# A list-scheduled attention and MLP kernel: the planner's lengths, its ranks, the order of transfers and the gates of the weights are replaced

## The chip, the core and the metric

The kernel runs on one core of a Trainium2 chip. A core has five engines that each run their own instruction queue strictly in order: TensorE (PE in the profile, with PEld for its weight loads), VectorE (DVE), ScalarE (ACT), GpSimd (POOL) and SyncE (SP), which here only issues DMAs. The engines meet through semaphores. DMA transfers run on 16 DMA engines beside them; SP's and ACT's go through one kind of queue (hardware_dynamic, q1 and q10 in the profile), POOL's through another (software_dynamic, q0). The metric is the device time of one execution in microseconds; the median of three runs is the kernel's time.

## What is computed

Four batches of eight heads, 768 positions, head size 64. Keys are cut into 24 chunks of 32. For each query an upper bound of its score with each chunk is worked out, the six best chunks that are not in the future are kept, and attention runs over those alone. The result, seen as 3072 tokens of 512 numbers, goes through an MLP with a hard-swish.

```python
ub = sum(max(q * k_min[chunk], q * k_max[chunk]))          # per query and chunk
ub = where(causal, ub, -1e9); top = argsort(ub)[..., -6:]
scores = where(sel & (pos_q >= pos_k), q @ k.T / 8, -1e9)
attn = softmax(scores) @ v                                  # -> x: 3072 x 512
h = x @ w_in                                                # 512 -> 2048
out = (h * clip(h + 3, 0, 6) / 6) @ w_out                   # 2048 -> 512
```

## The kernel before

**Tiling.** The 32 heads make 16 pairs, p0 to p15; a batch b has four pairs, and two pairs make a quad that is loaded together. The 768 positions are handled in two halves of 384. A unit is two pairs and one half: unit 0 is p0, p1 in half 0; unit 1 is p2, p3 in half 0; units 2 and 3 are their half 1; units 4 and 5 are p4, p5 and p6, p7 in half 0, and so on to unit 15.

**Attention of a pair and half.** K and Q are loaded by SP. In batch 0 the load is `load_quad` (L237, rows of 768 bytes) and TensorE turns the tile (`turn`, L377); in the other batches it is `load` (L246): four transfers, each into 32 of the 128 partitions in rows of 128 bytes, and VectorE turns the tile by a transpose over all 128 partitions (`turn_out`, L389), so that this transpose needs all four transfers. Then come the chunk limits (`limits`, L402 and L403 on VectorE, L405), GpSimd's copies of keys and queries (L340, `keys` and `queries`), the bounds (L442), the selection on VectorE (L447 to L472, `largest`, `select`, `select_out`), the scores (L495 for batch 0, L498 for the others), the exponentials (L508 on ScalarE), the causal triangle (L513 on GpSimd), the product with V (`values`, L529) and its division (`values_out`, L535 and L541 on VectorE). V is loaded at L252 (batch 0, three transfers) or L257 and cast by `cast_values`.

**MLP of a group.** A group g is a batch and a half, 384 tokens; g00 is batch 0, half 0. Its tokens are turned by TensorE (`turn_tokens`, L550, copied out at L554) for g00, g01 and g10, and by VectorE and a round trip through DRAM for the other five (`turn_words` L560, `keep_words` L565, `fetch_words` L571, `part_words` L579 on GpSimd). Then come 16 `hidden` blocks (L586, each followed by L591 on ScalarE and L594 on VectorE) and three `result` tiles of four parts (L601; the last tile of all at L609). Each `hidden`, `values`, `turn`, `turn_tokens` or `result` tile takes one of four PSUM banks ("m"), and gives it back when the engine that reads it is done.

**Weights.** `load_weights` issues four transfers of 1 MB on GpSimd's queue: I0 and I1, the halves of w_in (needed by `hidden` blocks 0 to 7 and 8 to 15), and O0 and O1, the halves of w_out. Ahead of each stands a copy of one element of an earlier transfer's tile (`seen`, L322): the gate. GpSimd stands still at it until that transfer has landed. I0 to O1 are issued in this order.

**What sets the order.** Nothing above is written in its final order. The function body only registers steps with `plan.add`: an engine or several to choose from, a length in microseconds, a rank, the steps it follows, and the buffers it takes and gives back. `Plan.order` then plays a list schedule: at each moment a free engine takes the ready step of lowest rank. The instructions are emitted in that order, engine by engine, so that the plan decides every queue, but at run time only the semaphores hold anything back. `SHIFT` adds a number to the ranks of about 200 steps. A transfer is given a length too, and is stretched by a share while weights are under way:

```python
weights = max(free["WT"] - now, 0.0) + sum(x["lengths"]["WT"] for x in ready["WT"])
length = min(length / st["share"], weights + max(length - st["share"] * weights, 0.0))
```

Of the kernel before, what the change touches and what calls it, by code (L numbers as in the profile page):

```python
# [46 lines left out]
class Plan:  # L47
# [8 lines left out]
    FETCH = 15.3, 1.35  # L56
# [36 lines left out]
    def order(self, **busy):  # L93
# [20 lines left out]
        while events:  # L114
            now, _, done, own = heapq.heappop(events)
            if done:
                behind(done, own)
                if not own:
                    for held in done["give"]:
                        held[1] -= 1  # L120
                        if not held[1]:
                            self.room[held[0]].append(held[2])
                            opened[held[0], held[2]] = now
            for e, steps in ready.items():
                if free[e] > now + 1e-9:
                    continue
                for st in sorted(steps, key=lambda x: x["rank"][:1] if e == "DMA" else x["rank"]):
                    if "engine" in st:
                        steps.remove(st)
                    elif self.sooner(st, e, free, now):  # L130
                        continue
                    elif self.room_for(st):
                        steps.remove(st)
                        for held in st["take"]:
                            held[2] = self.take(held[0])
                        st["idle"] = now - max([free[e], *(opened.get((held[0], held[2]), 0.0) for held in st["take"])])
                        out.append(st)
                        begin = now
                        if e == "POOL" or e == "DVE" and st["port"]:
                            begin = max(now, port["DVE" if e == "POOL" else "POOL"])  # L140
                            port[e] = begin + st["lengths"][e]
                        begin = max(begin, locks.get(st["lock"], 0.0))
                        if e == "PE":
                            begin += 0.1 * (st["tiles"] != tiles)
                            tiles = st["tiles"]
                        length = st["lengths"][e]
                        if e == "PE" and begin < self.COLD:
                            length *= 1.9
                        if e == "DMA":
                            weights = max(free["WT"] - now, 0.0) + sum(x["lengths"]["WT"] for x in ready["WT"])  # L150
                            length = min(length / st["share"], weights + max(length - st["share"] * weights, 0.0))
                            if now <= self.FETCH[0] < now + length:
                                length += self.FETCH[1]
                        st["at"], st["engine"], st["length"] = begin, e, length
                        free[e] = begin + st["length"]
                        if st["lock"]:
                            locks[st["lock"]] = free[e] + 0.12
                        n += 2
                        heapq.heappush(events, (free[e], n, st, True))
                        heapq.heappush(events, (free[e] + self.BEHIND[e], n + 1, st, False))  # L160
                        break
# [10 lines left out]
def kernel(  # L172
# [465 lines left out]
    GATE = dict(I0="V3", I1="I0", O0="K4", O1="I1")  # L638
# [34 lines left out]
    def load_input(n, name, after=()):  # L673
# [17 lines left out]
        elif half == 0:  # L691
            got = arrive("SP", 0.6, 1.35, (load, two, name, x), after=after, take=take, parts=4)
            for st in two:
                there[name, st["pair"], 0] = there[name, st["pair"], 1] = got
# [42 lines left out]
    def prepare(n):  # L737
# [11 lines left out]
        for st in two:  # L749
# [3 lines left out]
            for name, f in (("KS", "kf"), ("QS", "qf")):  # L753
# [3 lines left out]
                if first:  # L757
                    m = bank_of[name] = hold("m", 2 if name == "KS" else 1)
                    here = direct[name] = [add("PE", 0.4, r + lead, later(turn, st, name, half), after=here, take=[m], give=used)]
# [9 lines left out]
            else:  # L769
                masks_beside(p, r)  # L770
                made["K", p, half] = [add(dict(POOL=0.54), None, r + lead + 1, later(keys, st, half, j), port=True,
                                          after=[a] + free.get(("KL", p - 6), []), give=[held["kf"]]) for j in range(2)]
            b1 = add("DVE", 0.95 if first else 0.93, r + lead, later(limits, st, half, 0), after=(direct["KS"] if first else [a]) + free.get(("KM", p - 6), []),
# [11 lines left out]
            chain += [c, add(dict(ACT=0.45, DVE=0.33, POOL=0.6) if first else dict(ACT=0.42), None, r + lead, later(queries, st, half, "relu"), after=[c], port=True,  # L785
# [4 lines left out]
            made["Q", p, half] = [add(dict(POOL=0.54), None, r + lead + 1, later(queries, st, half, j), port=True,  # L790
# [17 lines left out]
    def attend(u):  # L808
# [8 lines left out]
        a = add("DVE", 0.36 if half == 0 else 0.53, r + RANK["sel"], later(select, u), after=[a] + selected.get(half, []), give=[ub], port=True)  # L817
# [3 lines left out]
        for j in range(2 if n >= 4 else 0):  # L821
            mask.append(add(dict(DVE=0.46, ACT=0.83, POOL=0.9), None, r + RANK["sel"] + j, later(masks_out, u, j), port=True,
# [3 lines left out]
        for i, st in enumerate(two):  # L826
# [6 lines left out]
            for t in range(tiles):  # L833
# [12 lines left out]
                for jb, q0, w, c0 in PLAN[half][t]:  # L846
                    if q0 == jb * P:
                        parts.append(add("POOL", 0.37, r + RANK["tri"], later(triangle, st, half, t, c0), after=[e]))
# [43 lines left out]
    for what in ("I0", "I1", "O0", "O1"):  # L892
        name, n = dict(I="WIN", O="WOUT")[what[0]], int(what[1])
        got, seen = landing[GATE[what]]
        there[name, n] = arrive("POOL", 0.95, 6.3 if name == "WIN" else 7.3, (load_weights, name, n, seen), after=got[-1:])
# [3 lines left out]
    for n_group, ((b, half), xs) in enumerate(finished.items()):  # L899
# [3 lines left out]
        if (b, half) in WORDS:  # L903
# [12 lines left out]
            for kt in range(KT_HID):  # L916
                xt.append(add("POOL", 0.55, r + RANK["rw"], later(part_words, g, kt), after=landed + xt[:1], take=[held_xt] if kt == 0 else [], give=[held_bf]))
# [6 lines left out]
        for f in range(FT):  # L924
# [3 lines left out]
            a = add("ACT", 0.48, r + RANK["fs"] * f + RANK["rt"], later(hidden_relu, g, f), after=before, take=[u])  # L928
            gts.append(add("DVE", 0.475, r + RANK["fs"] * f + RANK["rt"], later(hidden_out, g, f), after=[a], give=[m, u]))
# [59 lines left out]
```

## Time and profile before

| | us |
|---|---|
| median of 3 runs (range) | 271.57 (270.55 to 271.87) |
| profiled execution, its own time | 270.71 |
| its span | 269.0 |
| PE busy | 258.5 (96%) |
| DVE busy | 205.2 (76%) |
| ACT busy | 190.0 (71%) |
| POOL busy | 125.6 (47%) |

The page gives shares for the whole span, and the timeline, the waits and the DMA view can be asked for a stretch of it. A line of a timeline is start, duration, engine, source line, operation, output and inputs, and the number of instructions merged into it; in brackets stands the idle time before it and what ended that. A line of the DMA view is the queue, its packets, megabytes and the time of its packets as a share of the 16 DMA engines in the stretch; under "issues" the last number is the microseconds from issue to landing. The granted TensorE clock was 0.998.

### The profile page before, as it was taken

The numbers are of one execution on the slowest core, as the hardware profiler recorded it, in microseconds if no ns is written. First come the engines' busy times: TensorE is split into PE (matmuls) and PEld (weight loads), VectorE is DVE, ScalarE is ACT, GpSimd is POOL, SyncE is SP. The second block draws the span as 40 slices with busy tenths as digits, with TensorE's granted clock in tenths as the row PEclk, the third lists the DMA queues.
The fourth block names the chain that finished last, engine by engine and source line by source line (L and its number), as shares of the span: only waits on it lengthen the run. The fifth ranks groups of instructions, "written<-read, shape, count | busy, mean of one in ns | idle before, by whom it ended". The sixth has DMA issues, their size and how long they took to land.

```text
span 269.0 us, 6720 instructions
## 1 busy us (share of the span) xinstructions
PE 258.5 (96%) x2466; PEld 155.2 (58%) x2484; DVE 205.2 (76%) x582; ACT 190.0 (71%) x305; POOL 125.6 (47%) x284
## 2 busy tenths in 40 slices
PE   7998999999999999899999999999999999999994
PEld 5855666665445666554664566644666556645553
DVE  5789889889988698799889999979997126804800
ACT  3777899686457788764994499944997679716810
POOL 2547577005958559648845584772372221111000
PEclk9999999999999999999999999999999999999999
DMA  7999999999982999994999799223100420042012
GB/s 222 286 208 177 176 180 193 200 131 146 221 208 84 145 177 168 132 175 138 140 143 167 178 130 174 54 80 117 40 0 4 156 80 1 2 157 80 0 39 78
DMA packets 115329, 34.91 MB, mean 130 GB/s; under 512 B 100960, under 2 KB 110688, under 8 KB 115296
## 3 DMA queue, kind: packets, MB, share of 16 engines
q1 hardware_dynamic: 111616, 29.89, 60.3%
q0 software_dynamic: 3136, 4.19, 9.5%
q8 instruction: 19, 0.31, 0.5%
q10 hardware_dynamic: 544, 0.39, 0.5%
q14 instruction: 14, 0.11, 0.1%
HBM read 29.23 MB, written 8.26 MB: 139 GB/s over the span
## 4 chain that ended last, share of the span: by engine, by line
PE 73%; DVE 8%; DMA 7%; ACT 4%; SPq 3%; issue 1%; POOL 1%; ACTq 0%; DVEq 0%; POOLq 0%
PE OP L601 24%; PE HP L586 23%; PE SPS L498 6%; DMA KS<-in_k_dram 5%; PE PVP L529 5%; PE UBT L442 5%; PE SPS L495 3%; DVE GT L594 3%; ACT PT L508 3%; PE QT L377 2%; PE KT L377 2%; SPq L246 2%; PE OP L609 1%; DVE KF L389 1%; DMA BD<-BT 1%
## 5 line engine op out<-in xcount | busy, mean ns | idle before, releaser
L508 ACT ACTIVATE PT<-SPS 128x1024 bf16<-128x1024 f32 (+2 forms) x96 | 84.5, 927 | 11.6 <-PE SPS L498 7.9
L586 PE MATMUL HP<-XT,WIN 128*128 128x384 bf16 x512 | 90.1, 326 | 1.3 <-DVE Xb L541 0.8
L594 DVE SCALAR_TENSOR_TENSOR GT<-U,HP 128x384 bf16<-128x384 bf16 x128 | 67.2, 549 | 29.9 <-ACT U L591 25.6
L601 PE MATMUL OP<-WOUT,GT 128*128 128x512 bf16 x350 | 83.4, 379 | 1.2 <-issue 0.3
L591 ACT ACTIVATE U<-HP,THREE 128x384 bf16<-128x384 f32 x128 | 71.6, 594 | 8.1 <-PE HP L586 4.2
L586 PEld LDWEIGHTS <-WIN 128*128 128x128 bf16 x512 | 48.8, 98 | 32.6 <-issue 1.3
L513 POOL TENSOR_SCALAR_AFFINE_SELECT PT<-PT 128x256 bf16<-128x256 bf16 x96 | 39.6, 423 | 51.5 <-ACT PT L508 50.7
L601 PEld LDWEIGHTS <-GT 128*128 128x128 bf16 x368 | 34.7, 98 | 40.4 <-issue 3.7
L340 POOL TENSOR_SCALAR_AFFINE_SELECT QLA<-QF 64x384 bf16<-64x384 f32 x48 | 24.2, 506 | 24.6 <-DVE QF L389 18.9
L498 PE MATMUL SPS<-QLA,KL 128*128 128x384 bf16 (+2 forms) x240 | 35.5, 278 | 0.1
L627 ACT ACTIVATE OT<-OP 128x512 f32<-128x512 f32 x22 | 13.1, 594 | 30.0 <-PE OP L601 26.7
L498 PEld LDWEIGHTS <-KL 128*128 128x128 bf16 x240 | 21.4, 98 | 12.1 <-issue 0.3
L340 POOL TENSOR_SCALAR_AFFINE_SELECT KL<-KF 64x384 bf16<-64x384 f32 x48 | 24.1, 504 | 8.3 <-DVE KF L389 6.7
L529 PEld LDWEIGHTS <-PT 128*128 128x128 bf16 x672 | 24.3, 97 | 6.0 <-POOL PT L513 2.4
L529 PE MATMUL PVP<-VB,PT 128*128 128x65 bf16 x672 | 26.3, 193 | 1.2 <-POOL PT L513 1.1
L413 ACT ACTIVATE QR<-QF 128x384 f32<-128x384 f32 x29 | 14.5, 525 | 10.4 <-DVE QF L389 8.5
L541 DVE TENSOR_TENSOR Xb<-PVP,RINV 128x384 bf16<-128x384 f32 x32 | 18.5, 579 | 1.1
L579 POOL COPY XT<-BF 128x384 bf16<-128x384 bf16 x20 | 9.7, 523 | 14.9 <-DMA BF<-BD 14.8
L389 DVE STREAM_TRANSPOSE KF<-KS 128x384 f32<-128x384 f32 x24 | 13.2, 560 | 3.3 <-DMA KS<-in_k_dram 3.3
L266 POOL TENSOR_SCALAR_AFFINE_SELECT VB<-VT 128x768 bf16<-128x768 f32 x12 | 10.8, 908 | 6.4 <-DMA VT<-in_v_dram 4.3
L389 DVE STREAM_TRANSPOSE QF<-QS 128x384 f32<-128x384 f32 x24 | 12.3, 550 | 1.7 <-PE UBT L442 1.7
L402 DVE TENSOR_REDUCE KMA<-KF 128x12 f32<-128x384 f32 x24 | 13.1, 547 | 0.5
(75 smaller groups left out, 223.6 us busy)
## 6 DMA issues: line engine op xcount, KB each, us to landing
KS<-in_k_dram SPq DMA_DIRECT2D x31, 192.0 KB, 5.2
QS<-in_q_dram SPq DMA_DIRECT2D x31, 192.0 KB, 5.5
out_dram<-OT SPq DMA_DIRECT2D x23, 256.0 KB, 2.2
VT<-in_v_dram SPq DMA_DIRECT2D x24, 192.0 KB, 4.6
WIN<-in_moe_w_in_dram POOLq DMA_DIRECT2D x2, 1024.0 KB, 9.3
WOUT<-in_moe_w_out_dram POOLq DMA_DIRECT2D x2, 1024.0 KB, 13.0
BD<-BT SPq DMA_DIRECT2D x5, 384.0 KB, 2.3
BF<-BD SPq DMA_DIRECT2D x20, 96.0 KB, 2.3
```

The costliest lines, as they stand in the source:

```text
L340: nc.gpsimd.affine_select(out=to, in_=x, pattern=[[0, n]], compare_op=A.is_ge, fill=0.0, base=0, channel_multiplier=0)
L389: nc.vector.transpose(T[:], st[name][:, st["i"], half * HC:(half + 1) * HC, :].rearrange("p c e -> p (c e)"))
L413: nc.scalar.activation(QR[:], QF[:], ACT.Relu)
L498: nc.tensor.matmul(SP[:, j, c0:c0 + n], lhsT=KLS[st["pair"] % 6][:, j, jb * P:(jb + 1) * P], rhs=st["QL", half][:, j, at:at + n], start=Tr ...
L508: nc.scalar.activation(PT[:, :, 0:cols], SP[:, :, 0:cols], ACT.Exp, scale=scale)
L513: nc.gpsimd.affine_select(out=PT[:, :, c0:c0 + P], in_=PT[:, :, c0:c0 + P], pattern=[[0, 2], [1, P]], compare_op=A.is_ge, fill=0.0, base=0 ...
L529: nc.tensor.matmul(PVP[:, j, n, :], lhsT=PT[:, j, c0:c0 + P], rhs=st["VB"][:, jb, j, :], start=(jb == 0), stop=(jb == qb))
L541: nc.vector.tensor_tensor(out=to, in0=PVP[:, :, :, 0:D], in1=RINV[:].to_broadcast([P, 2, HB, D]), op=A.mult)
L586: nc.tensor.matmul(HP[:], lhsT=WIN[:, kt, f * P:(f + 1) * P], rhs=g["XT"][:, kt, :, :], start=(kt == 0), stop=(kt == KT_HID - 1))
L591: nc.scalar.activation(U[:], g["HP", f][:], ACT.Relu, bias=THREE[:], scale=1.0)
L594: nc.vector.scalar_tensor_tensor(out=g["GT"][:, f, :], in0=g["U", f][:], scalar=6.0, in1=g["HP", f][:], op0=A.min, op1=A.mult)
L601: nc.tensor.matmul(g["OP", t][:], lhsT=g["GT"][:, f, t * P:(t + 1) * P], rhs=WOUT[:, f, :], start=(f == 0), stop=(f == FT - 1))
```

## The change

No instruction's work changes, and there are as many DMAs. What changes is the numbers from which the order is made:

- lengths of steps: the turns of batch 0 (0.4 to 0.65), several of GpSimd's (`keys` and `queries` 0.54 to 0.5, `part_words` 0.55 to 0.47, the triangle 0.37 to 0.39), `select`, `masks_out`, `hidden_relu`, the issue of weights (0.95 to 1.05), the four-part load (1.35 to 1.4);
- the instruction fetches that the plan puts on the DMA engines: four moments in place of one;
- the table `SHIFT`, wholly;
- the gates of the weights. A letter and number is a load of that unit: K1 is K of unit 1.

```diff
-    FETCH = 15.3, 1.35
+    FETCH = 11.5, 59.5, 76.0, 92.0
...
-                            if now <= self.FETCH[0] < now + length:
-                                length += self.FETCH[1]
+                            for fetch in self.FETCH:
+                                if now <= fetch < now + length:
+                                    length += 1.2
...
-    GATE = dict(I0="V3", I1="I0", O0="K4", O1="I1")
+    GATE = dict(I0="K1", I1="V2", O0="Q3", O1="Q4")
...
-            got = arrive("SP", 0.6, 1.35, (load, two, name, x), after=after, take=take, parts=4)
+            got = arrive("SP", 0.6, 1.4, (load, two, name, x), after=after, take=take, parts=4)
...
-                    here = direct[name] = [add("PE", 0.4, r + lead, later(turn, st, name, half), after=here, take=[m], give=used)]
+                    here = direct[name] = [add("PE", 0.65, r + lead, later(turn, st, name, half), after=here, take=[m], give=used)]
...
-        there[name, n] = arrive("POOL", 0.95, 6.3 if name == "WIN" else 7.3, (load_weights, name, n, seen), after=got[-1:])
+        there[name, n] = arrive("POOL", 1.05, 6.3 if name == "WIN" else 7.3, (load_weights, name, n, seen), after=got[-1:])
...
-                xt.append(add("POOL", 0.55, r + RANK["rw"], later(part_words, g, kt), after=landed + xt[:1], take=[held_xt] if kt == 0 else [], give=[held_bf]))
+                xt.append(add("POOL", 0.47, r + RANK["rw"], later(part_words, g, kt), after=landed + xt[:1], take=[held_xt] if kt == 0 else [], give=[held_bf]))
```

The queues that come out of it differ nearly everywhere. The parts that matter below are these (K4a to K4d are the four transfers of K4; E4, E5 and E1 are copies by `beside`, L345; V0a to V0c are the parts of V0; "out g01.1" is the store of result tile 1 of g01).

```
SP before:  K2a Q1a Q1b Q2a Q3a K1a K1b K2b Q3b Q2b V0a V0b E5 V0c V2a V2b E4 E5 V3a K3a K3b V3b V3c
            V1a V1b V1c E4 V2c K4a K4b K4c K4d Q4a Q4b Q4c K6a K6b K6c Q6a Q4d K6d
SP after:   K1a Q1a Q1b V0a Q3a K2a K1b Q2a Q2b K2b Q3b E4 V2a V2b V0b V0c K3a K3b V3a V3b V3c E5 V1a
            V1b V1c V2c E4 K4a Q4a K4b K4c K4d Q4b Q4c V7a Q4d K6a K6b K6c E1 K6d

POOL before: ... triangles p0, p1 | I0 | triangles p2, p3, ... triangle p0 half 1 (3) | I1 |
             triangles p1 (2) | O0 | keys p4, p5 half 1 ... keys p5 half 0 | O1 | ...
POOL after:  queries p1 | I0 | ... triangles p0, p1, p2, p3 | I1 | triangle p0 half 1 (1) | O0 | ...
             keys p5, p4 ... triangles p3 half 1 | O1 | ...

DVE before, after values_out of p0 half 1:
             turn+limits p4, hidden 1, 0, turn+limits p5, hidden 3, 2, values_out p1, turn+limits p5, ...
DVE after:   hidden 0, 1, 2, 3, turn+limits p5, values_out p1, turn+limits p5, hidden 4,
             turn+limits p4, hidden 5, 6, turn+limits p4, hidden 7, values_out p2, hidden 8, 9, 10,
             values_out p3, then the first turned tokens of g01

PE after, from the same place: hidden 0 to 3 of g00, scores p2 (2), values p1, scores p2, hidden 4,
             scores p2, p3, hidden 5, 6, scores p3, values p2, ... values p3, hidden 11, 12,
             turn_tokens g01, hidden 13, turn_tokens g01, hidden 14, 15, then the 16 of g01

SP before, later: out g01.1, out g01.2, out g01.0, K8a to K8d, Q8a, V8, V9, K10a, V10a, out g00.1,
             V10b, K10b K10c K10d, Q8b ...
SP after:    out g01.0, out g00.2, out g01.1, V8a, K8a to K8d, out g01.2, Q8a, V8b, V9, K10a K10b K10c,
             out g00.1, K10d, V10, Q8b ...
```

More of the change, by code (lines that the diff above doesn't have):

```diff
@@ L770, in prepare @@
                 masks_beside(p, r)
-                made["K", p, half] = [add(dict(POOL=0.54), None, r + lead + 1, later(keys, st, half, j), port=True,
+                made["K", p, half] = [add(dict(POOL=0.5), None, r + lead + 1, later(keys, st, half, j), port=True,
                                           after=[a] + free.get(("KL", p - 6), []), give=[held["kf"]]) for j in range(2)]
-            b1 = add("DVE", 0.95 if first else 0.93, r + lead, later(limits, st, half, 0), after=(direct["KS"] if first else [a]) + free.get(("KM", p - 6), []),
+            b1 = add("DVE", 0.97 if first else 0.93, r + lead, later(limits, st, half, 0), after=(direct["KS"] if first else [a]) + free.get(("KM", p - 6), []),
                      give=[bank_of["KS"] if first else held["kf"]], lock=("KS", p, half) if first else None)
@@ L784, in prepare @@
                 u["qf", p][1] = 4
-            chain += [c, add(dict(ACT=0.45, DVE=0.33, POOL=0.6) if first else dict(ACT=0.42), None, r + lead, later(queries, st, half, "relu"), after=[c], port=True,
+            chain += [c, add(dict(ACT=0.45, DVE=0.33, POOL=1.05) if first else dict(ACT=0.42), None, r + lead, later(queries, st, half, "relu"), after=[c], port=True,
                              take=[u["qr", p]], give=[u["qf", p]])]
@@ L789, in prepare @@
                 continue
-            made["Q", p, half] = [add(dict(POOL=0.54), None, r + lead + 1, later(queries, st, half, j), port=True,
+            made["Q", p, half] = [add(dict(POOL=0.5), None, r + lead + 1, later(queries, st, half, j), port=True,
                                       after=[c] + free.get(("QL", n_queries - 7), []), give=[u["qf", p]]) for j in range(2)]
@@ L816, in attend @@
         a = add("DVE", 0.6 if half == 0 else 1.02, r + RANK["sel"], later(largest, u), after=[a])
-        a = add("DVE", 0.36 if half == 0 else 0.53, r + RANK["sel"], later(select, u), after=[a] + selected.get(half, []), give=[ub], port=True)
+        a = add("DVE", 0.4 if half == 0 else 0.6, r + RANK["sel"], later(select, u), after=[a] + selected.get(half, []), give=[ub], port=True)
         a = add("DVE", 0.55, r + RANK["sel"], later(select_out, u), after=[a], take=[mt])
@@ L821, in attend @@
         for j in range(2 if n >= 4 else 0):
-            mask.append(add(dict(DVE=0.46, ACT=0.83, POOL=0.9), None, r + RANK["sel"] + j, later(masks_out, u, j), port=True,
+            mask.append(add(dict(DVE=0.36, ACT=0.82, POOL=0.8), None, r + RANK["sel"] + j, later(masks_out, u, j), port=True,
                             after=[a] + mask + sum([free.get(("QL", st["q", half] - 6), []) for st in two], []), give=[mt]))
@@ L847, in attend @@
                     if q0 == jb * P:
-                        parts.append(add("POOL", 0.37, r + RANK["tri"], later(triangle, st, half, t, c0), after=[e]))
+                        parts.append(add("POOL", 0.39, r + RANK["tri"], later(triangle, st, half, t, c0), after=[e]))
             if st["b"] == 0:
@@ L927 @@
                           take=[m, held_gt] if f == 0 else [m], give=[held_xt])]
-            a = add("ACT", 0.48, r + RANK["fs"] * f + RANK["rt"], later(hidden_relu, g, f), after=before, take=[u])
-            gts.append(add("DVE", 0.475, r + RANK["fs"] * f + RANK["rt"], later(hidden_out, g, f), after=[a], give=[m, u]))
+            a = add("ACT", 0.49, r + RANK["fs"] * f + RANK["rt"], later(hidden_relu, g, f), after=before, take=[u])
+            gts.append(add("DVE", 0.48, r + RANK["fs"] * f + RANK["rt"], later(hidden_out, g, f), after=[a], give=[m, u]))
         for t in range(HB):
```

30 rows, old and new, of the table SHIFT are left out of this document.

## The prediction

> **What bounds the kernel now.** I read the page first, then who waits for whom on TensorE, then the chain that ended last.
>
> ```profile
> span 269.0 us, 6720 instructions
> PE 258.5 (96%) x2466; PEld 155.2 (58%) x2484; DVE 205.2 (76%) x582; ACT 190.0 (71%) x305; POOL 125.6 (47%) x284
> PE   7998999999999999899999999999999999999994
> ```
>
> ```profile
> PE SPS L495 <- ACT PT L508: 1.2, 2, 1.0
> PE PVP L529 <- POOL PT L513: 1.1, 2, 0.6
> PE HP L586 <- DVE Xb L541: 0.8, 1, 0.8
> PE HP L586 <- DVE GT L594: 0.4, 1, 0.4
> ```
>
> ```profile
> 51.21 11.80 PE HP L586 x72
> ...
> 261.53 3.51 PE OP L609 x32
> ```
>
> TensorE has work in 258.5 of 269.0 us. In the row of 40 slices its holes lie at the two ends, in the fourth (20 to 27 us) and in the seventeenth (108 to 114), and the four wait rows, 3.5 us together, are what it waits for between the ends. From 115 to 265 us it is dense. A new order of the same instructions can win at most these 3.5 us and what the start hides, and loses wherever a queue no longer keeps pace with TensorE. So I go through the stages in order of time, and ask in each what TensorE would now wait for.
>
> **Start, to 34 us.** I0, the first weights, moves from behind V3 to behind K1. Three views carry this. SP's timeline has the issues of K3a (13.92) and V2c (19.78), and the transfers issued then took 4.7 and 2.8 us:
>
> ```profile
> 13.92 0.98 SPq L237 DMA_DIRECT2D KS<-in_k_dram  x2
> 19.78 0.59 SPq L252 DMA_DIRECT2D VS<-in_v_dram  x1
> KS<-in_k_dram SPq DMA_DIRECT2D x1, 192.0 KB, 4.7
> VS<-in_v_dram SPq DMA_DIRECT2D x1, 128.0 KB, 2.8
> ```
>
> The packets of the two queues in 24 to 30 us, while I0 moves, and of SP's alone in 56 to 58:
>
> ```profile
> q0 software_dynamic: 515, 1.03, 98.9%
> q1 hardware_dynamic: 741, 0.09, 18.4%
> q1 hardware_dynamic: 2811, 0.36, 124.4%
> ```
>
> The timelines of TensorE and ScalarE where K3a is used:
>
> ```profile
> 21.29 0.88 PE L377 MATMUL KT<-IDENT,KS 128*64 128x128 f32 x12
> 22.22 0.48 ACT L262 CAST KL<-KT 128x384 bf16<-128x384 f32 x1 [0.69 <-PE KT L377]
> 30.90 2.85 ACT L508 ACTIVATE PT<-SPS 128x1024 bf16<-128x1024 f32 x3 [1.09 <-PE SPS L495]
> ```
>
> I0 holds the DMA engines for 6.0 us, and in them SP's queue moves 741 packets, which alone take 741/1405 = 0.5 us. So whatever SP has behind I0 comes 5.5 us later. K3a landed at 18.6, V2c eight places on at 22.6, 0.5 us a place. K3a now stands three places earlier and 5.5 us late: 22.6. TensorE would reach its turn 0.5 us sooner than 21.3 (one `values` less ahead), so it waits 1.8 us, and ScalarE, which sets the pace here, starts its cast some 1.4 us later. Its 1.09 us of idle at 30.9 take that up to 0.3. I take +0.3. Ends: -0.7 (nothing late, and the 0.69 at 22.2 used) and +1.8 (nothing taken up).
>
> **Weights against K4, 27 to 53 us.** This decides. GpSimd's timeline has the issue of I0, and the gate ahead of I1; then three single K transfers of the 128-byte form, one that met no weights (issued at 20.5), one that met I0 (23.1), one that met I1, O0 and O1 (34.4); then the packets from 43 to 46, while w_out moves; last the short stores at the end, which nothing disturbs:
>
> ```profile
> 22.09 1.00 POOL L325 DMA_DIRECT2D WIN<-in_moe_w_in_dram  x1
> 32.35 0.57 POOL L322 CAST seenWIN<-WIN 1x1 f32<-1x1 bf16 x1
> ```
>
> ```profile
> KS<-in_k_dram SPq DMA_DIRECT2D x1, 192.0 KB, 3.8
> KS<-in_k_dram SPq DMA_DIRECT2D x1, 192.0 KB, 11.0
> KS<-in_k_dram SPq DMA_DIRECT2D x1, 192.0 KB, 21.2
> q0 software_dynamic: 562, 0.58, 113.2%
> q1 hardware_dynamic: 563, 0.07, 30.4%
> out_dram<-OT SPq DMA_DIRECT2D x2, 128.0 KB, 1.7
> ```
>
> The two queues get one packet for one, 187 a us each, where SP's alone moves 1405. Before, I0 alone met K4, and I1 came when K4 was through. Now I1 waits for V2, whose last transfer stands right ahead of K4, and O0 follows I1 after one triangle.
>
> V2c: 22.6 + 5.5, less 0.2 to 1.0 for two `beside` copies that no longer stand ahead of it: it lands at L = 27.4. Gate 0.6 and the 1.8 us from issue to first packets (22.1 to 23.9) start I1 at L + 2.4 = 29.8; it moves till 35.8, and O0 (1 MB in packets of 1 KB, 187 a us) till 41.3. Behind V2c, SP's queue holds E4 (0.2) and K4a Q4a K4b K4c K4d, 1536 packets each (192 KB by 128 bytes), 1.09 us. Packets end 1.7 us ahead of a landing, by the short stores. Unheld, K4d would end at 27.4 - 1.7 + 0.2 + 5.5 = 31.4. At 29.8 about 2,200 packets of this are left: K4d and part of K4c. For K4d alone, 741 pass beside I1 and 795 beside O0, 4.3 us: it ends at 40.1 and lands at 41.8; for all 2,200 at 43.3. By the rows it was issued when its lane came free, about 26.5, and 3.8, 11.0 or 21.2 behind that are 30.3, 37.5 and 47.7: the ends. I take S = 42, nearest to the second and third, since two weight transfers meet it.
>
> What waits for S, by the timelines of TensorE, ScalarE and VectorE:
>
> ```profile
> 34.41 1.47 PE L586 MATMUL HP<-XT,WIN 128*128 128x384 bf16 x8
> 35.75 0.58 ACT L591 ACTIVATE U<-HP,THREE 128x384 bf16<-128x384 f32 x1
> 37.77 0.57 DVE L389 STREAM_TRANSPOSE KF<-KS 128x384 f32<-128x384 f32 x1
> ...
> 39.31 1.01 DVE L594 SCALAR_TENSOR_TENSOR GT<-U,HP 128x384 bf16<-128x384 bf16 x2
> 40.23 0.19 DVE L535 RECIPROCAL RINV<-PVP 128x6 f32<-128x6 f32 x1
> ...
> 40.93 0.57 DVE L389 STREAM_TRANSPOSE KF<-KS 128x384 f32<-128x384 f32 x1
> ```
>
> VectorE now has all four turns of K4 behind `hidden` 0 to 3 of g00. Four blocks of 0.65 (11.80/18) from 34.4 + 0.3 end at 37.3; ScalarE's 0.6 and VectorE's 0.5 make 38.4. There it meets K4d. Behind the turn stand `values_out` of p1 and `hidden` 4 and on; GpSimd's keys of p5 wait for it, and p2's triangles behind them; TensorE gets through `hidden` 6 and then stands for a PSUM bank. From the turn on, VectorE has four turns with limits (37.77 to 39.31: 1.54 each), three `values_out` (40.23 to 40.93: 0.70) and seven `hidden` (0.46): 11.5 us until g01's tokens can be turned, and some 2.8 us of turns, copies and blocks until g01's first. 38.4 + 14.3 = 52.7, where TensorE by itself would be at 51.2 + 1.3 + 0.3 = 52.8. There is no slack: what K4d lands beyond 38.4, TensorE is late. 42.0 - 38.4 = +3.6; ends 0 (37.5) and +9.3 (47.7).
>
> O1, now behind p3's triangles, has `hidden` of g01 to hide it: 0, and up to its 5.5 us if that cover were gone.
>
> **After 63 us.** The timelines of TensorE, SP and VectorE:
>
> ```profile
> 62.85 7.93 PE L601 MATMUL OP<-WOUT,GT 128*128 128x512 bf16 x35
> 79.73 5.85 SPq L633 DMA_DIRECT2D out_dram<-OT  x2
> 109.14 0.58 DVE L389 STREAM_TRANSPOSE KF<-KS 128x384 f32<-128x384 f32 x1 [2.38 <-DMA KS<-in_k_dram]
> ```
>
> SP stood at a store till 85.6 with K8 behind it; K10d landed just before 109.14 and held VectorE for 2.38 us, for which TensorE paid the 0.8 and 0.4 above. In the new order two result parts fewer (0.9 each) lie ahead of that store, and K10d stands two places further up: about 3 us sooner. The 1.2 us go. The 1.1 us behind GpSimd's triangles, which are late next, may go or stay; half of them makes -1.8, ends -2.4 and 0.
>
> Elsewhere TensorE has no wait to lose and can only find new ones, and four more warm-up matmuls stand in a gap of the start: together +0.3, ends 0 and +1.5.
>
> **Sum.** 0.3 + 3.6 - 1.8 + 0.3 = +2.4 on the profiled execution's own 270.71: 273.1. It stood 0.86 below the median; at the median the forecast is 274.0.
>
> **Rivals.** Faster: K4d slips through. No more than some 750 packets of it may be left when I1 starts (S = 38.4 is the point), so L would have to come one transfer sooner against I1. For it: idle in SP's queue that I0's hold would use up, and a landing that lags its packets by more than 1.7 us. Against: five transfers, 5.5 us, in a window of 2.4 + 1.7 us. Time on the median: 271.6 + 0.3 - 1.8 = 270.1, and 269.5 with all of the late gain. By the Trainium skill, "DMA: Bandwidth & Descriptors", section "Queues, rings and completion order", an engine takes its queues in turn and drains a whole packet, typically some 9 to 17 descriptors, before it switches; if a turn passed so many 128-byte rows against one of the weights', K4d would be hardly later than alone, and the time would be this rival's. The trace's 562 to 563 is against that, so it adds nothing to the chance.
>
> No change: K4d is held by I1 and a little of O0, S = 40: +1.6 for 3.6, and the late gain makes that up: 272.
>
> Slower still: K3a's wait is not taken up and nothing is won at 92 to 112: 1.5 and 1.8 us more, 277. Or K14's first transfer, which SP now issues between g20's store and its fetches, holds g20's tokens (1.1 us).
>
> The change does not do what it says: I0 not issued at K1, because GpSimd is busy. It is the least busy engine (47%); this would give the first rival's time.
>
> **How the numbers follow.** As forecast 0.48; slower still 0.08; no change 0.16; slipping through 0.28, with 0.03 for the late gate in it. A measurement of this kernel can tell about 0.5% (1.4 us) from no change. The first two are slower, the third the same, the fourth faster by that bound or just at it: 0.56, 0.16, 0.28. The range runs from the fourth's 269.5 to S = 45 with half of the late gain, 278; the forecast's own is 272.9 to 276.
>
> **What would show it.** I0 issued near 10 us, I1 near 28, O0 two to three us on. VectorE's first transpose of a K4 tile (L389) starts at 41 to 43 after some 3.6 us of idle on a KS transfer; TensorE waits at L529 or L586 for VectorE or GpSimd between 43 and 53; g01's first block starts at 56 instead of 52.5; no wait of VectorE's near 109. The forecast is wrong if that transpose starts by 38.5, or if TensorE waits after 115 us for something that it did not wait for.

## The result, and the profile after

| | before | after |
|---|---|---|
| median, us (range) | 271.53 (270.55 to 271.87) | 279.46 (278.28 to 279.65) |
| ratio to before (95% interval) | 1 | 1.0311 (1.0284 to 1.0338) |
| profiled execution, its own time | 270.71 | 279.29 |
| its span | 269.0 | 277.6 |
| PE busy | 258.5 | 261.3 |
| granted clock | 0.998 | 0.979 |

The change makes the kernel 7.9 us slower. The forecast was 2.4 us slower, 274.0, and at most 278. Here and below a ratio is made from the executions within 1.5% of the kernel's fastest; where others came out longer, the range shows them. Line numbers below are one less than before, since the change shortens the file by a line.

The page of the kernel after, then who waits for whom on TensorE:

```profile
span 277.6 us, 6734 instructions
PE   7998992499999999999999999999999999999994
PEclk9999999589999999999999999999999999999998
```

```profile
PE PVP L528 <- DVE Xb L540: 7.5, 1, 7.5
PE PVP L528 <- POOL PT L512: 1.2, 1, 1.2
PE KT L376 <- DMA KS<-in_k_dram: 0.3, 1, 0.3
```

The hole at 108 to 114 us is filled (TensorE is busy in all 6 us, where it was in 4.7); the one at 20 to 27 is still there (6.3 of 7 us, where it was 6.0). A new, deeper one stands in the seventh and eighth slices, 42 to 55 us, and the clock is low in the eighth. By stages, first the kernel before, then the one after (start:end, length, PE busy, instructions, granted clock, DMA share, GB/s):

```profile
0.00:40.00 40.00, 37.19 (x541) 1.00 1.05 208
40.00:65.00 25.00, 24.95 (x223) 1.00 1.24 166
92.00:115.00 23.00, 20.48 (x214) 1.00 1.10 157
```

```profile
0.00:40.00 40.00, 37.74 (x538) 1.00 0.99 203
40.00:65.00 25.00, 16.20 (x160) 0.80 1.06 141
92.00:115.00 23.00, 22.89 (x244) 1.00 1.04 159
```

TensorE is idle 0.55 us less before 40, 8.75 more from 40 to 65, 2.41 less from 92 to 115. That leaves +5.8; it is also busy 2.8 us longer, with the same work at a lower clock. Together 8.6, the difference of the spans. So one stage decides. Here are VectorE's timeline there, SP's, the end of SP's part in the chain of work that ended last, and GpSimd's timeline:

```profile
36.56 2.13 DVE L593 SCALAR_TENSOR_TENSOR GT<-U,HP 128x384 bf16<-128x384 bf16 x4 [1.94 <-ACT U L590]
48.59 0.58 DVE L388 STREAM_TRANSPOSE KF<-KS 128x384 f32<-128x384 f32 x1 [9.91 <-DMA KS<-in_k_dram]
```

```profile
24.34 0.54 SPq L245 DMA_DIRECT2D KS<-in_k_dram  x1
30.04 0.32 SPq L245 DMA_DIRECT2D QS<-in_q_dram  x1
30.41 13.88 SPq L245 DMA_DIRECT2D KS<-in_k_dram  x3
```

```profile
30.41 4.49 SPq L245
34.96 8.08 SPq L245
43.08 5.32 DMA KS<-in_k_dram
```

```profile
28.03 0.79 POOL L324 DMA_DIRECT2D WIN<-in_moe_w_in_dram  x1
29.48 0.40 POOL L512 TENSOR_SCALAR_AFFINE_SELECT PT<-PT 128x256 bf16<-128x256 bf16 x1 [0.66 <-ACT PT L507]
29.84 0.17 POOL L321 COPY seenWOUT<-QS 1x1 f32<-1x1 f32 x1
29.96 0.90 POOL L327 DMA_DIRECT2D WOUT<-in_moe_w_out_dram  x1
```

VectorE meets K4's first turn at 38.7 and stands 9.9 us for K4d, which is issued at 43.08 and lands at 48.40. The reason is first of all on SP. K4a is issued at 24.34, and then SP issues nothing until 30.04. Its waits name what it stood for, and the DMA rates in 40 slices of 26 to 32 us show the DMA engines empty from 27.5 to 29.5 but for one transfer:

```profile
SPq L245 <- POOL seenWOUT L321: 5.1, 1, 5.1
```

```profile
GB/s 207 199 196 183 118 44 31 20 15 5 0 0 0 0 109 0 0 0 0 0 0 0 0 96 82 41 55 27 41 109 109 150 150 137 177 205 218 205 137 191
```

`seenWOUT` is O0's gate. With `O0="Q3"` it copies one word out of the QS tile of Q3, so that tile isn't free before the copy. QS has two buffers, and Q4a, the first Q load of batch 1, takes this one. Q4a waits for GpSimd's copy, which stands in GpSimd's queue behind I1 and a triangle, and K4b, K4c and K4d stand behind Q4a on SP. The plan doesn't know of it: it books Q3's buffer against the turns alone, not against the gate's read. Seen from SP, O0's gate is no wait of O0 for Q3; it is a wait of K4 for O0.

When SP goes on, I1 and O0 are under way. From 38 to 41 us the queues move:

```profile
q0 software_dynamic: 544, 0.56, 109.9%
q1 hardware_dynamic: 544, 0.07, 30.3%
```

One packet for one, as forecast, 181 a us each, and SP spends 13.9 us issuing the three.

### The profile page after: what moved, and what is told of

It reads as the page before. It is cut to its first block, busy times and chain, and to the rows that moved or that the text cites. A ratio compares the mean times of both kernels' runs of the same rounds, so it can differ in the third digit from the quotient of the medians.

```text
span 277.6 us, 6734 instructions
## 1 busy us (share of the span) xinstructions
PE 261.3 (94%) x2467; PEld 157.0 (57%) x2488; DVE 205.9 (74%) x585; ACT 188.6 (68%) x303; POOL 121.6 (44%) x283
## 4 chain that ended last, share of the span: by engine, by line
PE 80%; DMA 7%; SPq 7%; ACT 2%; issue 1%; POOL 1%; DVE 1%; ACTq 0%; DVEq 0%; POOLq 0%
PE HP L585 29%; PE OP L600 28%; PE SPS L497 10%; PE PVP L528 6%; DMA KS<-in_k_dram 6%; SPq L245 5%; PE UBT L441 3%; ACT PT L507 1%; DMA QS<-in_q_dram 1%; PE OP L608 1%; SPq L251 1%; PE SPS L494 1%; SPq L236 1%; POOL PT L512 1%; PE XTP L549 0%
## 5 line engine op out<-in xcount | busy, mean ns | idle before, releaser
L507 ACT ACTIVATE PT<-SPS 128x1024 bf16<-128x1024 f32 (+1 forms) x96 | 85.1, 926 | 24.4 <-PE SPS L494 12.6
L585 PE MATMUL HP<-XT,WIN 128*128 128x384 bf16 x512 | 91.6, 328 | 0.0
L512 POOL TENSOR_SCALAR_AFFINE_SELECT PT<-PT 128x256 bf16<-128x256 bf16 x96 | 38.9, 418 | 44.0 <-ACT PT L507 43.2
L600 PEld LDWEIGHTS <-GT 128*128 128x128 bf16 x368 | 35.2, 98 | 38.7 <-issue 1.9
L339 POOL TENSOR_SCALAR_AFFINE_SELECT KL<-KF 64x384 bf16<-64x384 f32 x48 | 24.0, 501 | 29.4 <-DVE KF L388 27.5
L528 PE MATMUL PVP<-VB,PT 128*128 128x65 bf16 x672 | 26.7, 196 | 8.8 <-DVE Xb L540 7.5
L412 ACT ACTIVATE QR<-QF 128x384 f32<-128x384 f32 x32 | 16.4, 534 | 10.9 <-DVE QF L388 7.8
L401 DVE TENSOR_REDUCE KMA<-KF 128x12 f32<-128x384 f32 x24 | 13.1, 546 | 0.5
L402 DVE TENSOR_REDUCE KMA<-KF 128x12 f32<-128x384 f32 x24 | 13.0, 543 | 0.0
```

What stands on the lines that cost most here:

```text
L339: nc.gpsimd.affine_select(out=to, in_=x, pattern=[[0, n]], compare_op=A.is_ge, fill=0.0, base=0, channel_multiplier=0)
L412: nc.scalar.activation(QR[:], QF[:], ACT.Relu)
L507: nc.scalar.activation(PT[:, :, 0:cols], SP[:, :, 0:cols], ACT.Exp, scale=scale)
L512: nc.gpsimd.affine_select(out=PT[:, :, c0:c0 + P], in_=PT[:, :, c0:c0 + P], pattern=[[0, 2], [1, P]], compare_op=A.is_ge, fill=0.0, base=0 ...
L528: nc.tensor.matmul(PVP[:, j, n, :], lhsT=PT[:, j, c0:c0 + P], rhs=st["VB"][:, jb, j, :], start=(jb == 0), stop=(jb == qb))
L585: nc.tensor.matmul(HP[:], lhsT=WIN[:, kt, f * P:(f + 1) * P], rhs=g["XT"][:, kt, :, :], start=(kt == 0), stop=(kt == KT_HID - 1))
```

## The experiments

Two causes are on the table. Theory A: the hold of SP. Theory B: the weights' packets beside K4's, which was the forecast's term. All kernels take the plan of the changed kernel and move single steps in the list that it returns; `behind(i, j)` puts step i behind step j, and the diffs name the steps in words.

**The hold taken out.**

```diff
         got, seen = landing[GATE[what]]
+        seen = landing["V2"][1] if what == "O0" else seen
```

> The changed kernel, with one word changed: the copy that holds back O0 reads a word of VS (V2's) where it read one of QS (Q3's). Nothing moves in any queue. Theory A (the copy's read keeps Q3's buffer, and SP stands 5.1 us before Q4a with K4b to K4d behind it): Q4a is issued near 24.9 instead of 30.04, K4d near 30 instead of 43.08 and lands between 36 and 42, TensorE's idle 7.5 us near 43 falls below 4 us, 270 to 273 us. Theory B (the weights' packets beside K4's make it late, whatever SP does): K4d still lands after 46, and the time is above 277.

This takes 276.78 us, ratio 1.0214 (1.0188 to 1.0240). Here are the timelines of SP and VectorE, and the packets of 26 to 29.8 us and of 30 to 42:

```profile
25.27 0.86 SPq L245 DMA_DIRECT2D QS<-in_q_dram  x1
26.18 7.85 SPq L245 DMA_DIRECT2D KS<-in_k_dram  x3
```

```profile
45.58 0.58 DVE L388 STREAM_TRANSPOSE KF<-KS 128x384 f32<-128x384 f32 x1 [6.85 <-DMA KS<-in_k_dram]
```

```profile
q1 hardware_dynamic: 4312, 0.56, 143.9%
```

```profile
q0 software_dynamic: 1517, 2.05, 104.4%
q1 hardware_dynamic: 1617, 0.21, 21.0%
```

The hold is gone, but K4d comes only 3.0 us sooner. Theory A alone falls, and B's bounds (above 46, above 277) are just missed. The packets say why. Until I1 starts, SP's queue moves 4312 in 3.8 us, 1135 a us, so when I1 starts K4b is just through (it lands at 32.3) and K4c and K4d are still to come, and the weights' 12 us let 1617 packets pass.

**The hold kept, the weights late.**

```diff
+    lw = place("POOL", "load_weights", "WOUT", 0)
+    steps.insert(lw, <copy one word of Q3's QS tile>)
+    behind(I1, triangle p0 half 1, last)
+    behind(O0, triangle p1 half 1, second)
```

O0's own gate then reads V2's word, as above.

> The hold is kept: a copy of Q3's word stands in GpSimd's queue where O0's stood, so SP still waits for it till 30. But I1 and O0 are issued behind later masks, near 33 and 36 as in the kernel before. Theory A alone (the hold makes K4d late by itself): K4d lands after 43 and the time stays above 276. Theory B alone: K4b to K4d have the engines to themselves from 30.4 to 35, K4d lands by 38, TensorE's 7.5 us go, 268.5 to 271. If only the two together do it, this run and the first both come below 273.

This takes 276.06 us, ratio 1.0179 (1.0147 to 1.0212). Here are SP's waits and VectorE's timeline:

```profile
SPq L245 <- POOL hold L968: 5.1, 1, 5.1
```

```profile
43.74 0.58 DVE L388 STREAM_TRANSPOSE KF<-KS 128x384 f32<-128x384 f32 x1 [5.35 <-DMA KS<-in_k_dram]
```

Theory A's bounds are just met here (K4d lands at 43.5), but theory A alone fell in the first run; theory B alone falls here. So it is neither alone, and not "only the two together" either. K4d is issued at 31.9 and its packets are caught by I1, whose first are at 34.3.

**Both mended.** The first edit, and the two `behind` of the second.

> Both edits: O0's copy reads V2's word, and I1 and O0 are issued near 33 and 36. Both theories: K4d lands by 33, no idle of TensorE over 1 us near 43 to 55, granted clock 1.00 there; the change keeps its gains elsewhere (0.5 us before 40, 2.2 us between 95 and 115), so 268 to 269.5, faster than the kernel before by 2 to 3 us. If those gains came only from the idle time ahead of them, it is 271 to 272.

This takes 269.64 us, ratio 0.9946 (0.9923 to 0.9969): 1.5 us faster than the kernel before in the same runs (271.17), where 2 to 3 were expected. Here are VectorE's timeline and the stages:

```profile
38.66 0.57 DVE L388 STREAM_TRANSPOSE KF<-KS 128x384 f32<-128x384 f32 x1
```

```profile
0.00:40.00 40.00, 36.99 (x538) 1.00 1.06 207
40.00:65.00 25.00, 24.19 (x223) 1.00 1.21 170
92.00:115.00 23.00, 22.96 (x268) 1.00 1.13 159
```

K4d lands at 35.7, not by 33, but VectorE doesn't wait for it. The clock stays at 1.00, and 92 to 115 is full without a long idle time ahead of it: that gain, 2.5 us, belongs to the new order. The gain before 40 us isn't there (36.99 us busy, 37.19 in the kernel before), and from 40 to 65 us TensorE is idle 0.8 us more. In the table of two by two, the hold costs 2.7 us with the weights early (279.46 - 276.78) and 6.4 with them late (276.06 - 269.64); early weights cost 3.4 with the hold and 7.1 without. Each alone costs most of what both cost.

**SP's order alone.**

```diff
+    behind(Q4a, K4d)        # on SP; all gates as in the changed kernel
```

> The changed kernel with its gates as they are; in SP's queue alone Q4a goes from its place ahead of K4b to one behind K4d. The hold of SP is still there, with the rest of Q4 behind it. Theory A: K4d is issued near 27 and lands at 33 to 40, at most 2 us of idle near 43, 269 to 272. Theory B: K4d lands after 46, above 277.

VectorE's timeline:

```profile
40.22 0.58 DVE L388 STREAM_TRANSPOSE KF<-KS 128x384 f32<-128x384 f32 x1 [1.66 <-DMA KS<-in_k_dram]
```

Two executions take 268.81 and 269.22 us, ratio 0.9921 (0.9883 to 0.9959), with both the hold and the early weights still there: now Q4 is held, and nothing needs it soon. Three more took 273.8 to 275.1 at a granted clock of 0.985 to 0.994; no trace of them was kept, and whether K4d is later in them isn't settled. Theory A is right about the place. But the edit takes two things from ahead of K4b to K4d at once, the hold and Q4a's own 1,536 packets; with the hold alone taken out K4's turn came at 45.58. So this run shows that the order on SP is a cure, not that the hold is the only cause.

**One weight transfer at a time.** The first edit, and O0 to some 41 us, or I1 to 37:

```diff
+    behind(O0, triangle p2 half 1, first)     # free_i1_early
+    behind(I1, triangle p1 half 1, last)      # free_o0_early
```

> O0's copy reads V2's word, so SP isn't held; I1 stays early (28), O0 goes to some 41 us. By a count of packets, one for one: at I1's first packets (29.9) some 3,072 of K4c and K4d are left, 600 pass in I1's 6 us, 2,470 in 1.9 us behind it; K4d lands at 39.5 and the time is within 1 us of 270.7 (269.6 + 39.5 - 38.4). If I1 alone does the harm of both (its 2-KB packets), K4d lands after 43, at 274 or more.

> The same with the two exchanged: O0 stays early (near 30), I1 goes to some 37 us. By the count: O0's 1,024 packets let 1,024 of the 3,072 pass in 5.5 us, the rest goes in 1.6 us behind it: K4d lands at 39.2, 269.6 to 271.5. If O0 alone does the harm of both, K4d lands after 43, at 274 or more.

The first takes 269.42 us (268.15 to 272.33), ratio 0.9962 (0.9926 to 0.9998), the second 271.40 (268.92 to 278.39), 0.9993 (0.9954 to 1.0032). VectorE's timeline in the one and in the other:

```profile
38.69 0.58 DVE L388 STREAM_TRANSPOSE KF<-KS 128x384 f32<-128x384 f32 x1
```

```profile
41.23 0.58 DVE L388 STREAM_TRANSPOSE KF<-KS 128x384 f32<-128x384 f32 x1 [2.60 <-DMA KS<-in_k_dram]
```

K4d lands at 38.5 and 41.0, where the count of packets gave 39.5 and 39.2. Against the mended kernel, one transfer beside K4 costs 0 to 2 us; two in a row cost 7.

**What a late K4d costs.** The profiled executions in one table:

| kernel | first K4 turn | past 38.4 | own time | past 268.75 |
|---|---|---|---|---|
| changed | 48.59 | 10.2 | 279.29 | 10.5 |
| gate_reads_v2 | 45.58 | 7.2 | 276.57 | 7.8 |
| hold_kept_weights_late | 43.74 | 5.3 | 274.89 | 6.1 |
| free_o0_early | 41.23 | 2.8 | 271.25 | 2.5 |
| q4a_behind_k4d | 40.22 | 1.8 | 269.22 | 0.5 |
| free_i1_early | 38.69 | 0.3 | 268.15 | -0.6 |
| both_mended | 38.66 | 0.3 | 268.75 | 0 |

From 41 us on a microsecond of K4d is about a microsecond of the kernel. Each row is one execution, and those of the mended kernel alone range from 268.5 to 270.3.

**VectorE's order.** K4 as late as in the changed kernel; its turns with their limits and keys are moved behind ready work:

```diff
+    behind(turns, limits, keys of p5, values_out p2 half 1)
+    behind(turn, limits, keys of p4 half 0, hidden_out 8)
+    behind(turn, limits, keys of p4 half 1, hidden_out 10)
```

> The changed kernel with its transfers as they are (K4d late). Only VectorE's and GpSimd's order is edited: the four turns of K4 with their limits, and the keys made from them, stand behind work that is ready (hidden 4 to 9 of g00, values_out of p1 and p2, p2's triangles). If the late K4d costs what VectorE has left behind it (14.3 us, all behind S), some 3.3 us of that now fit into its wait of 9.9 us: 275.5 to 277, and TensorE's first wait falls from 7.5 to below 4.5 us. If what costs is the late keys of p4 and p5 themselves, whatever stands around them, the time stays within 1 us of the changed kernel's 279.5.

This takes 274.82 us, ratio 1.0139 (1.0105 to 1.0172). Here are VectorE's timeline and TensorE's waits:

```profile
48.89 0.58 DVE L388 STREAM_TRANSPOSE KF<-KS 128x384 f32<-128x384 f32 x1 [1.14 <-DMA KS<-in_k_dram]
```

```profile
PE PVP L528 <- POOL PT L512: 4.2, 1, 4.2
```

4.6 us better than the changed kernel with the same late K4d: more than the 3.3 counted. So nearly half of the 9.8 us that the hold and the early weights cost together is work that stood behind the turn on VectorE, or behind the keys on GpSimd, and had no need to. What is left shows as TensorE's wait for p3's triangles, which stand behind the keys on GpSimd.

**The clock.** 100 matmuls into the idle time:

```diff
+            if step is scores of p3, half 1, second:
+                idle[:] = [100]
```

> The changed kernel with 100 matmuls of 128 columns more, 5.8 us, ahead of the last scores before TensorE's idle 7.5 us; their results are overwritten. Nothing else moves. Theory C (the idle time lowers the granted clock, 0.50 from 50 to 55 us, and the slow matmuls cost 2 to 3 us beside the wait): granted clock 1.00 throughout and 276.5 to 277.5. Theory D (VectorE's 14.3 us behind K4d set the pace, and TensorE's slow matmuls hide beside them): clock 1.00, but 278.5 to 279.5. If the clock falls all the same, idle time is not its cause.

This takes 279.95 us, ratio 1.0331 (1.0298 to 1.0365). Here are TensorE's waits, and its windows from 53 us on:

```profile
PE PVP L528 <- DVE Xb L540: 1.9, 1, 1.9
PE PVP L528 <- POOL PT L512: 1.5, 2, 1.4
```

```profile
53.00:54.00 1.00, 0.50 (x11) 0.83 1.57 149
54.00:55.00 1.00, 1.00 (x17) 0.50 1.63 144
57.00:58.00 1.00, 1.00 (x12) 0.97 1.26 158
```

The low clock is shorter (53.7 to 57.1 us, 3.4 instead of 10) though not gone, and the time is no better, though K4's turn also came 0.4 us later here (49.03). This speaks for D: VectorE's work behind K4d sets the pace, and without the low clock the 2.8 us of longer busy time in the sum above would mostly be idle time. It isn't proof, as part of the dip is still there.

**The start, and O0 later still.** Both on the mended kernel:

```diff
+    behind(I0, triangle p1 half 0, last)      # both_mended_i0_late
+    behind(O0, triangle p2 half 1, first)     # both_mended_o0_later
```

> The mended kernel (269.6) with I0 issued near 23 us, behind p1's last triangle of its first half, as in the kernel before, instead of near 10. By the prediction's first step (the early I0 costs 0.3 us) it is 0.3 faster, 269.0 to 269.6. If the early I0 wins at the start (TensorE was 0.5 us less idle by 40 us), it is 270 to 270.5.

> The mended kernel with O0 issued near 41 us instead of 35.7, so that Q4's last two transfers (landed 49.1 and 51.2) meet I1 alone. Both should land by 46; VectorE's wait of 1.0 us at 51 for Q4d and TensorE's 0.8 us behind it go: 268.8 to 269.2. If O0 then meets the transfers of K6 and holds those, no gain or a loss up to 1 us.

The first takes 269.98 us, ratio 0.9980 (0.9946 to 1.0013), the second 270.43, 0.9973 (0.9946 to 1.0000). Both intervals overlap the mended kernel's. The early I0 may win up to 2 us; these runs don't tell it from nothing. O0's later place lets Q4c land at 43.6 instead of 49.1, but Q4d stays at 51.4 and VectorE waits 1.0 us for it as before: no gain.

## Why the prediction was wrong

**The start: +0.3, inside its ends, its sign not settled.** K3a landed at 21.5, not 22.6; TensorE waited 0.3 us for it, not 1.8, and was idle 0.55 us less by 40 us, inside the ends of -0.7 and +1.8. But in the ten traces here with I0 early TensorE is busy from 36.99 to 38.00 of these 40 us, with 37.19 in the kernel before, so 0.55 lies within the spread. Moving I0 back was not distinguishable either.

**Weights against K4: the step that failed.** The forecast took K4d to land at 42; it landed at 48.4. Two terms in it were wrong.

- "By the rows it was issued when its lane came free, about 26.5": it was issued at 43.08, and at 29.20 with the hold taken out. The gate was costed as a wait of GpSimd alone. What it reads, how long that holds a buffer, and who takes that buffer next were not asked. Taking the hold out brought 3.0 us of K4d back (48.59 to 45.58), 2.7 us of the time.
- "1.09 us" a transfer and "about 2,200 packets left": SP's queue moved 1135 packets a us there, not 1405, which makes 1.35 us a transfer, and K4c was still whole when I1 started. 3,072 packets were left; 1,617 went beside the weights and the rest after them. That is the other 3.4 us, from 42 to 45.4. The 1.7 us by which packets were to end ahead of a landing stand in rows that give the whole time from issue to landing, so they are an upper end of it.

The rest of the step held. I1 was issued at 28.03 and O0 at 29.96 (forecast 28 and two to three on); VectorE met K4's turn at 38.7 (38.4); the queues shared one for one, 544 to 544; TensorE waited at `values`; and from 41 us on every microsecond of K4d cost about one. I1's 28 is luck in part: V2c landed at 26.7, not 27.4, and the gate then stood behind a cast and triangles on GpSimd until 27.91. With 48.6 in place of 42 the step gives +10.2, and the sum is 0.3 + 10.2 - 1.8 + 0.3 = +9.0; 8.6 was measured on the profiled executions. The Trainium skill's 9 to 17 descriptors a turn ("DMA: Bandwidth & Descriptors", "Queues, rings and completion order"), by which K4d would have slipped through if a turn passed so many of its rows against one of the weights', don't show so here: 1,517 to 1,617 packets over 12 us. Whether the engines change queue at every packet or after as many of each, such sums can't tell.

**After 63 us: -1.8, right but small.** TensorE's idle time between 92 and 115 us went nearly wholly, 2.4 us of 2.5, the end of the range given. No new wait of TensorE's came up after 115.

**The sum without K4.** 0.3 - 1.8 + 0.3 = -1.2 was forecast for everything else; the mended kernel, which has everything else, is 1.5 us faster than the one before.

**The rivals.** "K4d slips through" had its price right (269.5 to 270.1; the mended kernel takes 269.64) and its point too (38.4), but not its condition: it asked for packets that get through in time, and the mended kernel had to free SP and move the weights. "Slower still" named K3a and K14, and neither shows in TensorE's waits. No rival asked whether SP itself could be held.

## What to carry to other kernels

A gate that reads a word of a tile is a reader of that tile: it keeps the buffer, and whoever takes the buffer next waits for the engine that does the gating. Gate on something whose buffer nobody wants soon, or put the transfer that takes the buffer behind those that are urgent. And when two causes make one transfer late, taking out either shows a third of the loss; try both before calling either small.

## What was not expected of the hardware

The granted clock falls soon, and without a long stand. In the changed kernel (its windows):

```profile
47.00:48.00 1.00, 0.00 (x0) 0.75 1.03 101
57.00:58.00 1.00, 1.00 (x9) 0.63 0.98 147
```

A mean of 0.75 is half a microsecond at 0.50: it fell at 47.5, 4.0 us after TensorE stopped, and came back at 57.7, 4.7 us after TensorE was busy without a break (53.1). This agrees with the Trainium skill, "TensorE: Matmul & The Clock Gate", section "Part 1: The HAM clock gate": free-running windows of about 3.4 us, one idle to close the gate and one busy to open it. But in the kernel with O0 alone early TensorE was idle for only 1.7 us in three pieces, and the clock fell all the same (timeline, then windows):

```profile
43.60 0.25 PE L528 MATMUL PVP<-VB,PT 128*128 128x65 bf16 x3 [0.16 <-DVE Xb L540]
44.03 0.33 PE L528 MATMUL PVP<-VB,PT 128*128 128x65 bf16 x5 [0.18 <-POOL PT L512]
45.70 1.33 PE L528 MATMUL PVP<-VB,PT 128*128 128x65 bf16 x22 [1.35 <-POOL PT L512]
```

```profile
45.00:46.00 1.00, 0.30 (x7) 0.90 1.24 200
46.00:47.00 1.00, 1.00 (x21) 0.50 0.60 95
49.00:50.00 1.00, 1.00 (x11) 0.89 0.85 124
```

By that rule, a whole idle window, the clock should have stayed up here; the measurement decides. A single wait of 1.30 us, in the mended kernel with I0 late, left it at 1.00. What share of a window has to be idle isn't shown by these runs.
